# Fewer numerators among gate/up chunks, and a first down pair that projects last: a gated mix of linear attention and a GEGLU block

## Chip, cores, metric

One core of one Trainium2 chip. The metric is device time in microseconds of one execution. Profile times are microseconds from the start of the profiled span, which is about 1.3 us shorter than the device time. In profile lines PE is TensorE's matmuls, PEld its weight loads, DVE VectorE, ACT ScalarE, SPq SyncE issuing a DMA, and L726 line 726 of the kernel.

## The reference, cut to what matters

```
x: (1, 2048, 640) bf16; 32 heads of 20; F = 1728
g = sigmoid((x * gate_w).sum(-1))
a = o @ wo,  o = num / den,  num = phi_q @ kv          # linear attention, phi = softmaxes of +pq and -pq
b = (gelu(x @ w_gate) * (x @ w_up)) @ w_down           # GEGLU block
out = g * a + (1 - g) * b
```

Of the kernel before, what the change touches and what calls it, by code (L numbers as in the profile page):

```python
# [107 lines left out]
class _Kernel:  # L108
# [6 lines left out]
    NFC = 14  # L115
# [235 lines left out]
    def mm(self, bank, c0, n, lhs, rhs, first, fin, reads):  # L351

        for a, z in ((0, 64), (64, P)) if self.columns else ((0, P),):
            self.sc.op("pe", lambda e: e.matmul(  # L354
                self.ps[a:z, bank * 512 + c0:bank * 512 + c0 + n], lhs[:, a:z], rhs, start=first, stop=fin),
                reads=reads, writes=[("ps", bank)], signal=fin and z == P)
# [345 lines left out]
        sc.dma("sp", lambda e: e.dma_start_transpose(self.goT[:, gs, :, :], self.Og[:, sl, :]),  # L702
               reads=[("Og", sl)], writes=[("goT", gs)], guard=old)

    def down_pair(self, t0, banks, widths):

        sc = self.sc
        ts = (t0, t0 + 1)
        NFC, KD = self.NFC - 1, self.KD
        nw = len(widths)  # L710
        hk = t0 // 4
        last = t0 + 2 == self.NT
        os_ = t0 % 4

        def mm(r, j, h, c, opens, x, n):
            t = ts[j]
            tt, gs, bk, w0, a = t % 4, t % 8, banks[h][j], sum(widths[:h]), 64 * r
            w, end = widths[h], x == n - 1
            if c <= NFC:
                lhs, rhs = self.hT(hk, c)[a:a + 64, tt * P:(tt + 1) * P], self.wd_sb[a:a + 64, c, w0:w0 + w]  # L720
                rd = [("hT", hk, c), "wd"] if c < NFC else [("hT", hk, 13, r), ("wd13", r)]
            else:
                k = c - NFC - 1
                lhs, rhs = self.goT[a:a + 64, gs, k, :], self.wo_sb[a:a + 64, k, w0:w0 + w]
                rd = [("goT", gs), "wo"]
            sc.op("pe", lambda e: e.matmul(self.bank(bk, w), lhs, rhs, start=opens and x == 0, stop=end and not opens,  # L726
                                           skip_group_check=True),
                  reads=rd, writes=[("ps", bk)] + ([("turn", bk)] if end else []), signal=end,
                  after=[("turn", bk)] if x == 0 and not opens else ())

        def evac(h):
            w0, w = sum(widths[:h]), widths[h]
            for j in (0, 1):
                bk, dst, g = banks[h][j], self.outsb[:, os_ + j, w0:w0 + w], self.Gm[:, ts[j]:ts[j] + 1]
                rd, wr = [("ps", bk), "Gm"], [("outsb", os_ + j, h)]
                if last and j == 1:
                    sc.op("dve", lambda e: e.tensor_scalar(dst, self.bank(bk, w), g, None, op0=ALU.mult), reads=rd, writes=wr)
                else:
                    sc.op("act", lambda e: e.activation(dst, self.bank(bk, w), AF.Copy, scale=g), reads=rd, writes=wr)  # L739
            if last:  # L740
                hs, c0, c1 = [h], w0, w0 + w
            elif h == nw - 1:
                hs, c0, c1 = range(nw), 0, self.D
            else:
                return
            if t0 < self.TB:
                rows = self.out[0:self.BT, :].rearrange("(p j) n -> p j n", j=self.TB)[:, t0:t0 + 2, :]
            else:
                rows = self.out[t0 * P:(t0 + 2) * P, :].rearrange("(j p) n -> p j n", p=P)
            sc.dma("sp", lambda e: e.dma_start(rows[:, :, c0:c1], self.outsb[:, os_:os_ + 2, c0:c1]),  # L750
                   reads=[("outsb", os_ + j, k) for j in (0, 1) for k in hs], writes=[("out", t0, h)])

        wos = [NFC + 1 + k for k in range(KD)]
        opening = list(range(NFC + 1)) + wos
        for part in (range(NFC + 1), range(NFC + 1, len(opening))):
            for h in range(nw):
                for x in part:
                    for r in (0, 1):
                        mm(r, r, h, opening[x], True, x, len(opening))
                    yield None  # L760
        closing = list(range(NFC)) + wos
        for h in range(nw):
            for x, c in enumerate(closing):
                for r in (0, 1):
                    mm(r, 1 - r, h, c, False, x, len(closing))
                if c == closing[-1]:
                    evac(h)
                yield None

    NUMB = 2  # L770
    oldk = [("Ek", k, r) for k in range(4) for r in (0, 1)] + [(w, k) for w in ("Dk", "Rk") for k in range(4)] + [
# [3 lines left out]
    def ffn(self):  # L775
        self.gn = 0
        self.pn = 0
        pairs = [(0, 1), (6, 7)]

        def gateups(b, after):  # L780
            for idx, c in enumerate([0, 1, 13] + list(range(2, 13))):
                self.gateup(b, c, pairs[self.pn % 2])
                self.pn += 1
                after(idx)

        def downs(b, side):
            p = [pairs[(self.pn + k) % 2] for k in (0, 1)]
            n = 0
            for t in (4 * b, 4 * b + 2):
                final = t + 2 == self.NT  # L790
                for _ in self.down_pair(t, p + [(2, 3)] if final else p, (256, 256, 128) if final else (320, 320)):
                    n += 1
                    if n in side:
                        self.num(side[n])

        def state(idx):
            if idx < 3:
                self.gram(13 + idx)
            if idx == 2:
                self.columns = False  # L800
                self.kv_evac()
                self.gates()
                self.kv_ones()
            if 6 <= idx < 11:
                self.kv_mask(idx - 6)

        def first_nums(idx):
            if idx in (4, 8):
                self.num(idx // 4 - 1)

        def none(idx):
            pass
        at = (1, 31, 61, 91)
        gateups(0, state)
        gateups(1, first_nums)
        gateups(2, none)
        gateups(3, none)
        for b in range(self.NB):
            downs(b, {at[k]: 4 * b + 2 + k for k in range(4 if b < 3 else 2)})


def bass_gated_mix__linear_kernel_hedgehog__geglu_ffn__prompt_kernel(
# [41 lines left out]
```

## The kernel before, where the change touches it

After the attention state is built, the kernel runs four blocks of gate/up (512 tokens each, matmuls over all 128 rows), then four down phases of four 128-token tiles. A *numerator* is what one tile needs of `phi_q @ kv`: 20 matmuls over 64 rows into PSUM banks 2 to 5, eleven VectorE instructions that end in `Og`, and one DMA transpose of `Og` into `goT`. The output projection of that tile (`wo` steps) reads `goT`.

A down phase has two *tile pairs* of 74 *steps* each. A step is two matmuls of 64 rows and 320 columns, one in each row half of TensorE, working at the same time on two PSUM banks. In the second half of a pair the row halves swap tiles, and so banks. A matmul that enters a swapped bank waits until the other half's last one there is complete (`after=turn`).

```
# numerators: two among gate/up block 1, the others inside down phases
def first_nums(idx):
    if idx in (4, 8):
        self.num(idx // 4 - 1)
at = (1, 31, 61, 91)
for b in range(self.NB):
    downs(b, {at[k]: 4 * b + 2 + k for k in range(4 if b < 3 else 2)})   # step -> tile

# one tile pair (down_pair): steps 0..NFC are down, wos the output projection
opening = list(range(NFC + 1)) + wos
for part in (range(NFC + 1), range(NFC + 1, len(opening))):
    for h in range(nw):                  # h: which bank pair (320 columns each)
        for x in part:
            for r in (0, 1):
                mm(r, r, h, opening[x], True, x, len(opening))
            yield None
closing = list(range(NFC)) + wos
for h in range(nw):
    for x, c in enumerate(closing):
        for r in (0, 1):
            mm(r, 1 - r, h, c, False, x, len(closing))    # row halves swapped
        if c == closing[-1]:
            evac(h)
        yield None
# ... (cut)
```

The softmax here doesn't subtract the row's maximum and nothing guards it: scores larger than these inputs give would overflow.

## Time and profile before

| | |
|---|---|
| time, median of 6 runs | 287.47 us (287.15 to 288.72) |
| profiled span | 286.2 us, clock 1.000 |
| TensorE busy | 281.8 us (98%), 98% of the chain that ended last |
| numerator among gate/up | costs TensorE 0.60 us |
| numerator in a down phase | costs TensorE 0.39 us |
| step in a down phase | 0.136 us |

TensorE bounds the kernel, and it hardly ever waits. So each instruction added to it, and each wait, goes into the time at full size. Another engine or a DMA matters only where TensorE waits for it. The lines behind the table are in the prediction (timelines: start, duration, what). One more line of the before profile also belongs here: VectorE's timeline at tile 3's sum (columns: start, duration, what, idle time before it and its releaser).

```profile
206.96 0.49 DVE L699 TENSOR_TENSOR Og<-O,O 128x640 bf16<-128x640 bf16 x1 [0.44 <-DVE O L697]
```

Other such sums start 0.09 us after the instruction before them; this one pauses 0.44. Before the change nobody waited for it.

### The profile page before, as it was taken

How to read it: one execution, taken by the hardware profiler on the slowest of the kernel's cores; microseconds unless marked ns; L12 is line 12 of the kernel's file. 1: busy time of each engine (PE TensorE's matmuls, PEld its weight loads, DVE VectorE, ACT ScalarE, POOL GpSimd, SP SyncE). 2: the span in 40 equal slices, each digit the busy share in tenths (PEclk: the TensorE clock that was granted, in tenths of full speed). 3: DMA queues.
4: the chain of work that ended last, by engine and by line, in shares of the span. 5: the costliest groups of instructions: out<-in, count | busy, mean ns of one | idle time of the engine just before them, and what ended most of it. 6: DMA issues, size and time to landing. Idle time of an engine off the chain costs nothing.

```text
span 286.2 us, 7006 instructions
## 1 busy us (share of the span) xinstructions
PE 281.8 (98%) x3017; PEld 186.7 (65%) x3032; DVE 174.9 (61%) x353; ACT 104.5 (37%) x199; POOL 5.3 (2%) x36
## 2 busy tenths in 40 slices
PE   8999999999999999999999999999999999999996
PEld 5566789999994444444444444445777777777785
DVE  2349999999976652567242334225883883883801
ACT  3367897678653222222323223221112112112111
POOL 7000000000000000000000000000000000000000
PEclk9999999999999999999999999999999999999999
DMA  8999996000002000011000000000232132222221
GB/s 226 206 176 236 367 366 201 0 2 2 2 0 48 0 0 0 3 24 23 2 0 0 0 2 0 0 0 2 25 84 62 45 48 81 61 49 72 70 72 48
DMA packets 36937, 18.67 MB, mean 65 GB/s; under 512 B 28970, under 2 KB 36394, under 8 KB 36906
## 3 DMA queue, kind: packets, MB, share of 16 engines
q1 hardware_dynamic: 36240, 18.19, 25.6%
q8 instruction: 24, 0.39, 0.6%
q10 hardware_dynamic: 666, 0.03, 0.2%
q14 instruction: 7, 0.06, 0.1%
HBM read 9.04 MB, written 2.62 MB: 41 GB/s over the span
## 4 chain that ended last, share of the span: by engine, by line
PE 98%; issue 0%; ACT 0%
PE ps L354 61%; PE ps L726 28%; PE ps L670 2%; PE ps L366 2%; PE ps L461 2%; PE ps L334 1%; PE ps L550 1%; PE ps L293 1%; ACT outsb L739 0%; PE ps L316 0%
## 5 line engine op out<-in xcount | busy, mean ns | idle before, releaser
L354 PE MATMUL ps<-xT,wg_sb 128*128 128x512 bf16 (+1 forms) x265 | 63.8, 379 | 0.4 <-issue 0.2
L354 PE MATMUL ps<-xT,wu_sb 128*128 128x512 bf16 (+1 forms) x263 | 63.3, 379 | 0.5 <-DVE hT L644 0.2
L642 ACT ACTIVATE gl<-ps 128x512 bf16<-128x512 f32 x52 | 30.9, 596 | 73.1 <-PE ps L354 68.7
L644 DVE TENSOR_TENSOR hT<-ps,gl 128x512 bf16<-128x512 f32 x39 | 26.7, 690 | 38.6 <-PE ps L354 38.5
L726 PE MATMUL ps<-wd_sb,hT 64*128 64x320 bf16 x648 | 48.5, 296 | 0.0
L354 PEld LDWEIGHTS ps<-xT,wu_sb 128*128 128x128 bf16 (+1 forms) x270 | 26.5, 99 | 29.8 <-DVE hT L644 0.5
L354 PEld LDWEIGHTS ps<-xT,wg_sb 128*128 128x128 bf16 (+1 forms) x270 | 26.2, 99 | 29.0 <-ACT gl L642 0.2
L354 PE MATMUL ps<-w,xT 128*64 128x512 bf16 (+6 forms) x398 | 41.5, 325 | 0.1
L739 ACT ACTIVATE outsb<-ps,Gm 128x320 bf16<-128x320 f32 (+2 forms) x31 | 14.5, 515 | 72.4 <-PE ps L726 72.4
L726 PEld LDWEIGHTS ps<-wd_sb,hT 64*128 64x128 bf16 x648 | 31.1, 94 | 12.2 <-issue 0.4
L354 PEld LDWEIGHTS ps<-w,xT 128*64 128x64 bf16 (+1 forms) x400 | 35.9, 107 | 4.5
L726 PE MATMUL ps<-wo_sb,goT 64*128 64x320 bf16 (+2 forms) x340 | 26.5, 288 | 0.0
L354 PE MATMUL ps<-xT,wq 128*64 128x512 bf16 (+1 forms) x184 | 26.0, 380 | 0.1
L431 DVE TENSOR_REDUCE Dk<-Ek 128x64 f32<-128x1280 bf16 x16 | 23.7, 1479 | 3.6 <-ACT gcol L419 3.6
L445 DVE TENSOR_TENSOR Ek<-Ek,Dk 128x640 bf16<-128x640 bf16 x32 | 25.0, 821 | 0.6
L697 DVE TENSOR_TENSOR O<-ps,RH 128x640 bf16<-128x640 f32 x32 | 24.8, 816 | 0.0
L416 ACT ACTIVATE Ek<-ps 128x640 bf16<-128x640 f32 x32 | 20.7, 703 | 4.2 <-PE ps L354 4.2
L530 ACT ACTIVATE Eq<-ps 128x512 bf16<-128x512 f32 x40 | 21.6, 607 | 0.6 <-PE ps L354 0.4
L644 DVE TENSOR_TENSOR xT<-ps,gl 128x512 bf16<-128x512 f32 x13 | 9.0, 691 | 18.2 <-PE ps L354 18.2
L726 PEld LDWEIGHTS ps<-wo_sb,goT 64*128 64x128 bf16 x340 | 16.0, 94 | 5.3
L354 PEld LDWEIGHTS ps<-xT,wq 128*64 128x64 bf16 (+1 forms) x185 | 15.4, 108 | 2.9
L726 PE MATMUL ps<-wd_sb,xT 64*128 64x320 bf16 (+2 forms) x270 | 16.0, 269 | 0.0
(69 smaller groups left out, 174.8 us busy)
## 6 DMA issues: line engine op xcount, KB each, us to landing
out_dram<-outsb SPq DMA_DIRECT2D x7, 320.0 KB, 2.3
wd_sb<-in_B_w_down_dram SPq DMA_DIRECT2D x1, 2080.0 KB, 13.9
wg_sb<-in_B_w_gate_dram SPq DMA_DIRECT2D x1, 1120.0 KB, 6.2
wu_sb<-in_B_w_up_dram SPq DMA_DIRECT2D x1, 1120.0 KB, 9.8
wg_sb<-in_B_w_gate_dram SPq DMA_DIRECT2D x1, 960.0 KB, 9.8
wu_sb<-in_B_w_up_dram SPq DMA_DIRECT2D x1, 960.0 KB, 10.2
w<-in_A_wqkv_dram SPq DMA_DIRECT2D x5, 160.0 KB, 4.0
wo_sb<-in_A_wo_dram SPq DMA_DIRECT2D x1, 800.0 KB, 9.2
```

What stands on the lines that cost most here:

```text
L354: self.sc.op("pe", lambda e: e.matmul(self.ps[a:z, bank * 512 + c0:bank * 512 + c0 + n], lhs[:, a:z], rhs, start=first, stop=fin), reads=r ...
L366: sc.op("pe", lambda e, c0=c0, n=n, bk=bk, col=col: e.matmul(self.bank(bk)[:, col:col + n], self.xT[:, kt, t * P:(t + 1) * P], self.w3[:, ...
L416: self.sc.op("act", lambda e, s=s, scale=scale: e.activation(self.Ek[:, se, s, :], self.ps[:, o:o + self.D], AF.Exp, scale=scale), reads=[ ...
L431: sc.op("dve", lambda e: e.tensor_reduce(self.Dk[:, se, 0, :].rearrange("p (s h) -> p s h", h=H), self.Ek[:, se, :, :].rearrange("p s (h d ...
L445: sc.op("dve", lambda e, v=v, r=r: e.tensor_tensor(v, v, r, ALU.mult), reads=[("Rk", se)], writes=[("Ek", se, s)])
L461: sc.op("pe", lambda e: e.matmul(self.ps[a:a + 64, b * 512 + c:b * 512 + c + 2 * nf], va[:, lo:lo + 64], self.Ek[:, se, :, f0:f0 + nf], st ...
L530: sc.op("act", lambda e, s=s, scale=scale: e.activation(self.Eq[:, s, i, b * self.BT:(b + 1) * self.BT], self.bank(bank), AF.Exp, scale=sc ...
L642: sc.op("act", lambda e: e.activation(self.gl[:, slot, :], self.bank(banks[0]), AF.Gelu_apprx_tanh), reads=[("ps", banks[0])], writes=[("g ...
L644: sc.op("dve", lambda e: e.tensor_tensor(hT, self.bank(banks[1]), self.gl[:, slot, :], ALU.mult), reads=[("ps", banks[1]), ("gl", slot)], ...
L697: dve(lambda e, o=o, f=f, s=s: e.tensor_tensor(o, V[s][:, :, :, 0:DH], f, ALU.mult), rb + [key(6 + s)], [("O", s, sl)], guard=old)
L726: sc.op("pe", lambda e: e.matmul(self.bank(bk, w), lhs, rhs, start=opens and x == 0, stop=end and not opens, skip_group_check=True), reads ...
L739: sc.op("act", lambda e: e.activation(dst, self.bank(bk, w), AF.Copy, scale=g), reads=rd, writes=wr)
```

## The change

Intent: only one numerator stays among gate/up, where it costs two changes of TensorE's tiling mode. The first down phase takes five numerators. So that tile 1 is in time there, the first tile pair takes all its down steps first and its output projection last ("late").

```
+        down = (list(range(NFC + 1)), list(range(NFC)))
+        def leg(h, half, cs, first, fin, enter, leave):
+            for x, c in enumerate(cs):
+                for r in (0, 1):
+                    mm(r, (r, 1 - r)[half], h, c, first and x == 0, fin and x == len(cs) - 1,
+                       enter and x == 0, leave and x == len(cs) - 1)
+                if fin and x == len(cs) - 1:
+                    evac(h)
+                yield None
+        if late:
+            for half in (0, 1):
+                for h in range(nw):
+                    yield from leg(h, half, down[half], half == 0, False, half == 1, True)
+            for h in range(nw):
+                yield from leg(h, 0, wos, False, False, True, True)
+                yield from leg(h, 1, wos, False, True, True, True)
+        else:
+            ... (the old order, in legs; cut)
...
-                for _ in self.down_pair(t, ..., (256, 256, 128) if final else (320, 320)):
+                for _ in self.down_pair(t, ..., (256, 256, 128) if final else (320, 320), t == 0):
...
-            if idx in (4, 8):
-                self.num(idx // 4 - 1)
+            if idx == 4:
+                self.num(0)
...
-        at = (1, 31, 61, 91)
+        at = (1, 31, 61, 91, 121)
+        nums = ((1, 2, 3, 4, 5), (6, 7, 8, 9), (10, 11, 12, 13), (14, 15))
-            downs(b, {at[k]: 4 * b + 2 + k for k in range(4 if b < 3 else 2)})
+            downs(b, dict(zip(at, nums[b])))
```

More of the change, by code (lines that the diff above doesn't have):

```diff
@@ L703, in num, with down_pair @@
                reads=[("Og", sl)], writes=[("goT", gs)], guard=old)
-    def down_pair(self, t0, banks, widths):
+    def down_pair(self, t0, banks, widths, late):
         sc = self.sc
@@ L713, in down_pair, with mm @@
         os_ = t0 % 4
-        def mm(r, j, h, c, opens, x, n):
+        def mm(r, j, h, c, start, stop, enter, leave):
             t = ts[j]
             tt, gs, bk, w0, a = t % 4, t % 8, banks[h][j], sum(widths[:h]), 64 * r
-            w, end = widths[h], x == n - 1
+            w = widths[h]
             if c <= NFC:
@@ L725, in mm @@
                 rd = [("goT", gs), "wo"]
-            sc.op("pe", lambda e: e.matmul(self.bank(bk, w), lhs, rhs, start=opens and x == 0, stop=end and not opens,
+            sc.op("pe", lambda e: e.matmul(self.bank(bk, w), lhs, rhs, start=start, stop=stop,
                                            skip_group_check=True),
-                  reads=rd, writes=[("ps", bk)] + ([("turn", bk)] if end else []), signal=end,
-                  after=[("turn", bk)] if x == 0 and not opens else ())
+                  reads=rd, writes=[("ps", bk)] + ([("turn", bk)] if leave else []), signal=leave,
+                  after=[("turn", bk)] if enter else ())
         def evac(h):
@@ L753, in down_pair @@
         wos = [NFC + 1 + k for k in range(KD)]
-        opening = list(range(NFC + 1)) + wos
-        for part in (range(NFC + 1), range(NFC + 1, len(opening))):
-            for h in range(nw):
-                for x in part:
-                    for r in (0, 1):
-                        mm(r, r, h, opening[x], True, x, len(opening))
-                    yield None
-        closing = list(range(NFC)) + wos
-        for h in range(nw):
-            for x, c in enumerate(closing):
+        down = (list(range(NFC + 1)), list(range(NFC)))
+        def leg(h, half, cs, first, fin, enter, leave):
+            for x, c in enumerate(cs):
                 for r in (0, 1):
-                    mm(r, 1 - r, h, c, False, x, len(closing))
-                if c == closing[-1]:
+                    mm(r, (r, 1 - r)[half], h, c, first and x == 0, fin and x == len(cs) - 1, enter and x == 0,
+                       leave and x == len(cs) - 1)
+                if fin and x == len(cs) - 1:
                     evac(h)
                 yield None
+        if late:
[6 more added lines that the diff above has]
+        else:
+            for h in range(nw):
+                yield from leg(h, 0, down[0], True, False, False, False)
+            for h in range(nw):
+                yield from leg(h, 0, wos, False, False, False, True)
+            for h in range(nw):
+                yield from leg(h, 1, down[1] + wos, False, True, True, True)
     NUMB = 2
@@ L790, in downs @@
                 final = t + 2 == self.NT
-                for _ in self.down_pair(t, p + [(2, 3)] if final else p, (256, 256, 128) if final else (320, 320)):
+                for _ in self.down_pair(t, p + [(2, 3)] if final else p, (256, 256, 128) if final else (320, 320),
+                                        t == 0):
                     n += 1
```

## The prediction

> **What bounds the kernel now**
>
> I read the page first (busy shares, then the chain that ended last), then the PE timeline around one numerator among gate/up and around those in the first down phase, then the VectorE and SyncE timelines for what a numerator's result goes through.
>
> Page, busy time by engine, and the chain:
>
> ```profile
> PE 281.8 (98%) x3017; PEld 186.7 (65%) x3032; DVE 174.9 (61%) x353; ACT 104.5 (37%) x199; POOL 5.3 (2%) x36
> ...
> PE 98%; issue 0%; ACT 0%
> ```
>
> TensorE is busy 98% of 286.2 us and carries 98% of the chain. The clock row is 9 throughout. So only three things count: TensorE cycles added or removed, and waits of TensorE. There is hardly a wait to win back, so a large gain is excluded from the start: 2% would be 5.75 us.
>
> PE timeline around the numerator that the change takes out of gate/up (the second one there):
>
> ```profile
> 126.91 1.03 PE L354 MATMUL ps<-xT,wu_sb 128*128 128x512 bf16 x4
> 127.87 0.56 PE L670 MATMUL ps<-KV,Eq 64*128 64x88 bf16 x20
> 128.37 0.82 PE L354 MATMUL ps<-xT,wg_sb 128*128 128x512 bf16 x3
> ```
>
> Gate/up matmuls start every 0.216 us (five take 1.24 us, the last of them 0.379). The last one before the numerator starts at 127.56, so without it the next would start at 127.78; it starts at 128.37, and its successor 0.226 instead of 0.216 later. The numerator costs 0.60 us here.
>
> Chain in order of time, first down phase:
>
> ```profile
> 197.61 0.24 PE ps L726 x2
> 197.85 0.39 PE ps L670 x20
> 198.24 4.08 PE ps L726 x60
> 202.32 0.39 PE ps L670 x20
> 202.71 4.07 PE ps L726 x60
> 206.78 0.39 PE ps L670 x20
> 207.18 4.08 PE ps L726 x60
> 211.25 0.39 PE ps L670 x20
> 211.64 7.88 PE ps L726 x116
> ```
>
> There it costs 0.39 us. A "step" (two concurrent 64-row matmuls) takes 4.08 / 30 = 0.136 us. No gap: TensorE waits for nothing, and one numerator to the next is 4.46 us.
>
> What becomes of a numerator (numbers of the one at step 61 of this phase, which is tile 4 before): PE, VectorE, SyncE timelines.
>
> ```profile
> 206.62 0.56 PE L670 MATMUL ps<-KV,Eq 64*128 64x88 bf16 x20
> 207.37 0.36 DVE L686 RECIPROCAL RH<-ps 128x32 f32<-128x32 f32 x1
> 209.44 1.55 DVE L697 TENSOR_TENSOR O<-ps,RH 128x640 bf16<-128x640 f32 x2
> 211.08 0.49 DVE L699 TENSOR_TENSOR Og<-O,O 128x640 bf16<-128x640 bf16 x1
> 211.64 1.20 SPq L702 DMA_TRANSPOSE goT<-Og  x1
> 212.97 0.71 PE L726 MATMUL ps<-wo_sb,goT 64*128 64x320 bf16 x8
> ```
>
> Its four banks are free after 209.44 + 1.55 = 210.99, 4.37 us after its start; its transpose is issued 5.02 us after its start. The sixteen transposes land 2.6 us after issue at the least and in the median, 4.2 at most (those of the first down phase: 3.6, 2.6, 2.6, 2.6). So a tile is ready for the output projection no sooner than 5.02 + 2.57 = 7.59 us after its numerator started. The last line is where the second tile pair of the phase (tiles 2 and 3) begins its output projection.
>
> **What the Trainium skill says**
>
> "TensorEngine Tiling (Array Packing)", Key Properties: a change of tiling mode drains TensorE. Gate/up is 128 rows, numerators and down steps 64, so a numerator among gate/up pays two switches; the trace agrees: 0.60 against 0.39 us. The same page, Gotcha 1, says that row tiles must not access one PSUM bank at the same time and that software must see to it: this is what the wait on "turn" is for, when the two row halves swap banks. "TensorE: Matmul & The Clock Gate", Single matmul latency, gives (398 + N) / 2.4 ns warm, 299 ns for N = 320; the trace's row has 296. "DMA: Bandwidth & Descriptors", the anatomy of one DMA, puts about 2 us of fixed cost on each DMA, mostly the write receipt; the transposes' 2.6 us agree, and say that the landing cannot be hurried.
>
> **The change part by part**
>
> No arithmetic is added or removed: the same sixteen numerators, the same matmuls. ACT's order stays; TensorE, VectorE and SyncE get a new order.
>
> 1. One numerator (tile 1) goes from gate/up into the first down phase: 0.60 - 0.39 = **-0.21 us**. The numerator that stays in gate/up is the one that also makes TensorE wait for VectorE (0.17 us, at 124.5), so that small wait is not won back.
>
> 2. The first tile pair now takes its down steps for both halves, then per bank pair the projection of half 0 directly followed by that of half 1. Half 1 swaps the banks between the row tiles, so its first weight load waits for the last matmul of half 0, just issued. Before, there were always at least five steps (0.68 us) between such a pair, over twice the latency. Estimate: 0.296 (matmul) + 0.054 (semaphore to weight load, as VectorE's end at 124.47 to the load at 124.52) + 0.01 for the unprefetched load, less the 0.136 that would pass anyway: 0.22 to 0.24 each, at steps 60 and 70. Two: **+0.47 us**.
>
> 3. All numerators slip by one place: tile 1 at step 1, 2 at 31, 3 at 61, 4 at 91, 5 at 121. The pair of tiles 2 and 3 still projects from step 103. Before, tile 3 was at 31, 72 steps ahead; now it is at 61. Between lie 41 steps (5.56), the numerator itself and that at step 91 (0.78): 6.34 us, plus the second turn wait 0.24 = 6.58 us. Needed: 7.59 + 0.05 = 7.64. TensorE waits 1.06 us. The same read off the lines above: the transpose of step 61 is issued at 211.64 and lands at 214.21, the projection starts at 212.97 + 0.24. **+1.06 us**.
>
> 4. Five numerators make the distance between the one at step 121 and the first of the next phase 28 steps (27 left of 148, and one): 28 x 0.136 + 0.39 = 4.19 us. The next needs the banks: 4.37 + 0.05 = 4.42 plus a short reload. Every other distance is 30 steps (4.46) or more, which just suffices. **+0.24 us**.
>
> 5. Tile 1 itself: needed from step 55, in the before timeline at 205.67 (its "late" form is there to buy this time); transposed from 202.66, landed at 205.23 if it takes 2.57: slack 0.4. With the 3.6 us that the transpose at that very place took before, TensorE would wait 0.6. In the DMA packets of the trace that transpose overlaps a 16 KB instruction fetch of TensorE (203.4 to 204.7); the slow ones of later phases do so too. One numerator less ahead of the phase puts that fetch 40 instructions later, ten steps (1.36 us), just behind the transpose's packets. I allow a quarter of 0.6: **+0.15 us**.
>
> Tile 5, 55 steps ahead of its use, has 8.5 us: no wait. Evacuation of the first pair's bank pair 0 now ends 10 steps (1.4 us and more) before those banks open again, ACT needs 1.0: no wait.
>
> Sum: -0.21 + 0.47 + 1.06 + 0.24 + 0.15 = +1.71. 287.44 + 1.7 = **289.1 us**, slower by 0.6%.
>
> **The rivals**
>
> A: the order was chosen well and only part 1 and the pairs' waits count, i.e. tile 3 is in time. For it: the "late" form shows that the author minded readiness. Against: it is applied to the first pair alone, and 6.6 us are less than the shortest chain of 7.64 that the trace has. It would give 287.44 - 0.2 + 0.5 + 0.2 = 287.9.
>
> B: transposes run into instruction fetches. 4.2 us in place of 2.57 for tile 3 and 3.6 for tile 1 would add 1.6 and 0.6: 290.6 to 291.2. For it: four of sixteen transposes took 3.9 us or more and three others 3.2 to 3.6. Against: the fetch near step 91 should come after that numerator, about 211.9 to 213.1 with the turn waits, mostly ahead of tile 3's packets (213.1 to 214.0).
>
> C: the mode switch costs more than the gap shows, or the remaining numerator's VectorE wait goes too: at most 0.4 more gained, 288.7.
>
> D: the turn waits are cheaper, because the modelled ends of matmuls overstate the latency. Half of 0.47 goes, but part 3 then waits 0.1 longer: 288.9.
>
> **Range and chances**
>
> Parts 1, 2 and 4 are uncertain by some 0.3 us together, part 3 by -0.3 and +1 (fetch), and runs of the same kernel on another chip by about 0.3. So 288.1 to 290.3 at 8 in 10, with more room above than below. To be 2% faster 5.75 us would have to go, of which TensorE has nothing to give; 2% slower takes three waits as large as part 3. Faster 0.005, within 2% 0.98, slower 0.015.
>
> **What would show it right or wrong**
>
> The PE chain of the changed kernel should have: one numerator in gate/up at the same 0.6 us, and 0.6 us less in gate/up; two gaps of 0.1 us or less in busy time, seen as 0.37 instead of 0.14 between starts, inside the first pair's projection; a wait of about 1 us of the projection of tiles 2 and 3 for the transpose (busy time shows some 0.2 less of it, as ends are modelled); about 0.2 us before the first numerator of the second down phase, released by VectorE's line 697 (or its new number). Second to fourth phases keep 21.7 us each. If no wait stands before tiles 2 and 3's projection, part 3 is wrong and rival A holds; if it is 2 us or more, rival B does; if the span falls, my account of what TensorE waits for is wrong altogether.

## The result, and the profile after

290.93 us in the median of 6 runs (290.58 to 292.26), against 287.47 of before: slower, clear of noise, though by less than 2%; ratio 1.0115 (95% interval 1.0087 to 1.0143). The direction was right; the size was not: +3.5 us instead of +1.7, and above the range's upper end of 290.3.

The TensorE timeline of the changed kernel in the first down phase (columns as before; lines left out):

```profile
196.78 0.56 PE L670 MATMUL ps<-KV,Eq 64*128 64x88 bf16 x20
...
204.76 0.30 PE L726 MATMUL ps<-wo_sb,goT 64*128 64x320 bf16 x1
206.02 1.35 PE L726 MATMUL ps<-wo_sb,goT 64*128 64x320 bf16 x13 [0.96 <-DMA goT<-Og]
207.21 0.56 PE L670 MATMUL ps<-KV,Eq 64*128 64x88 bf16 x20
...
213.83 0.30 PE L726 MATMUL ps<-wo_sb,goT 64*128 64x320 bf16 x1
215.48 1.53 PE L726 MATMUL ps<-wo_sb,goT 64*128 64x320 bf16 x19 [1.36 <-DMA goT<-Og]
```

Two waits for transposes stand here. At 204.76 the first row half, which needs tile 0, starts its projection alone; the second, which needs tile 1, starts at 206.02. Normally the two start 0.003 us apart, so TensorE lost 1.25 us. At 213.83 the same happens with tiles 2 and 3: 1.65 us. (The brackets say less, because a matmul counts as busy until its modelled end.)

The waits of TensorE in the changed kernel that the list of before did not have (waiter <- released by: us in all, times, longest; other lines left out):

```profile
PEld ps L726 <- DMA goT<-Og: 3.0, 2, 1.7
PE ps L726 <- DMA goT<-Og: 2.3, 2, 1.4
PEld ps L726 <- PE ps L726: 0.8, 2, 0.4
PEld ps L670 <- DVE O L697: 0.4, 1, 0.4
```

The third line is the two bank-swap waits. In the starts of the matmuls they are gaps of 0.356 and 0.387 us where 0.133 to 0.136 is usual: 0.22 and 0.25 lost. The fourth is the numerator after the one at step 121, whose banks VectorE had not yet emptied: 0.333 instead of 0.136, 0.20 lost.

VectorE at tile 3's sum, and the chain that ended last from there, in order of time (start, us, what):

```profile
212.01 0.49 DVE L699 TENSOR_TENSOR Og<-O,O 128x640 bf16<-128x640 bf16 x1 [0.44 <-DVE O L697]
```

```profile
211.58 0.43 issue
212.01 0.51 DVE Og L699
...
212.58 2.86 DMA goT<-Og
215.44 0.04 issue
215.48 2.66 PE ps L726 x37
```

The chain now runs through the pause of 0.43 us, the sum and the transpose, before it reaches TensorE. It is the same pause, at the same tile, as before; now somebody waits for it.

The query for the transpose of tile 1 alone answers with its time from issue to landing, first in the changed kernel:

```profile
L702 SPq DMA_TRANSPOSE goT<-Og x1: 1202/1202/1202, 201.8 to 201.8; - x1
...
  PEld ps L726: 1.3, 1
  PE ps L726: 1.0, 1
...
DMA to landing us min/median/max: 4.2/4.2/4.2
```

It was issued at 201.82 and landed at 205.97. This is what the DMA queues started between 203.95 and 204.95: one 16 KB packet of instructions, and three small packets.

```profile
## 3 DMA queue, kind: packets, MB, share of 16 engines
q8 instruction: 1, 0.02, 5.8%
q1 hardware_dynamic: 3, 0.00, 0.6%
```

The profile does not name the engine that the 16 KB packets are for. They are taken for TensorE's, because one comes for every 255 of its instructions in the mean. In the trace's packets this fetch starts 2.14 us after the transpose's issue and takes 0.94. Each transpose has 672 small packets of its own. Undisturbed they run from 1.17 to 2.12 us after issue, and the transpose lands 0.43 to 0.51 us after the last. Here 669 of them had started by 2.13; the last three are those in the view, and they started 3.06 to 3.10 us after issue, as the fetch ended. The transpose landed 1.03 us after the last of them. So 1.0 of its 1.6 us of delay is packets that came only behind the fetch; why the landing then took another 0.5 longer, the trace does not show.

The account of the two profiled runs, in us: numerator out of gate/up -0.60; the same numerator in the down phase +0.39; tile 1's wait +1.25; bank swaps +0.47; tile 3's wait +1.65; numerator at the phase's end +0.20. That is +3.36. In this run the changed kernel reached its first numerator 0.30 sooner and its last output store was 0.14 shorter, which change from run to run. Total +2.9; the spans (289.2 and 286.2) differ by 3.0.

### The profile page after: what moved, and what is told of

It is laid out like the page before. It is cut to its first block, busy times and chain, and to the rows that moved or that the text cites. A ratio compares the mean times of both kernels' runs of the same rounds, so it can differ in the third digit from the quotient of the medians. Undisturbed runs are those within 1.5% of the kernel's fastest.

```text
span 289.2 us, 7022 instructions
## 1 busy us (share of the span) xinstructions
PE 283.3 (98%) x3032; PEld 186.3 (64%) x3032; DVE 175.1 (61%) x353; ACT 104.6 (36%) x199; POOL 5.3 (2%) x36
## 3 DMA queue, kind: packets, MB, share of 16 engines
HBM read 9.04 MB, written 2.62 MB: 40 GB/s over the span
## 5 line engine op out<-in xcount | busy, mean ns | idle before, releaser
L354 PE MATMUL ps<-xT,wg_sb 128*128 128x512 bf16 (+1 forms) x270 | 64.9, 379 | 0.0
L354 PE MATMUL ps<-xT,wu_sb 128*128 128x512 bf16 (+1 forms) x270 | 64.8, 379 | 0.0
L726 PE MATMUL ps<-wd_sb,hT 64*128 64x320 bf16 x648 | 48.8, 296 | 0.0
L726 PEld LDWEIGHTS ps<-wd_sb,hT 64*128 64x128 bf16 x648 | 31.4, 94 | 12.1 <-issue 0.4
L726 PE MATMUL ps<-wo_sb,goT 64*128 64x320 bf16 (+2 forms) x340 | 27.4, 288 | 2.5 <-DMA goT<-Og 2.3
L726 PEld LDWEIGHTS ps<-wo_sb,goT 64*128 64x128 bf16 x340 | 16.0, 94 | 8.9 <-DMA goT<-Og 3.0
L726 PE MATMUL ps<-wd_sb,xT 64*128 64x320 bf16 (+2 forms) x270 | 16.0, 269 | 0.0
```

The lines of the kernel that those rows point to most:

```text
L354: self.sc.op("pe", lambda e: e.matmul(self.ps[a:z, bank * 512 + c0:bank * 512 + c0 + n], lhs[:, a:z], rhs, start=first, stop=fin), reads=r ...
L726: sc.op("pe", lambda e: e.matmul(self.bank(bk, w), lhs, rhs, start=start, stop=stop, skip_group_check=True), reads=rd, writes=[("ps", bk)] ...
```

## The experiments

Two theories of tile 1's 4.2 us were set against each other. F: a fetch of TensorE's instructions that falls into a transpose delays its landing. P: the first transpose of a down phase is slow at that place, whatever fetches do. Instructions added to TensorE's warm-up at the very start shift all later fetches without changing any work that counts: in the warm-up the engine only runs while the first loads arrive. "Tile 1's wait" and "tile 3's wait" below are excess gaps between the starts of TensorE's matmuls in the profiled run.

### Fetches shifted

```
-for n in (512, 512, 512, 512, 512, 512, 128):      # warm-up matmuls, columns each
+for n in (64,) * 50:                               # shift86: 86 instructions more
+for n in (128,) * 25:                              # shift36: 36 more
+for n in (32,) * 100:                              # shift186: 186 more
+for n in (512, 512):                               # warm2: 10 fewer
```

Control, the kernel before with 86 more:

> The kernel before with TensorE's warm-up in 50 matmuls of 64 columns instead of 7 of up to 512: 86 instructions more ahead of everything, no other work. A control. Theory F (a 16 KB instruction fetch of TensorE that falls between about 0.4 and 2.2 us after a transpose's issue delays its landing) and theory P (the first transpose of a down phase is slow at that place whatever the fetch does) both expect the time of before, 287.4 within 0.4 us, as nothing waits there. F: the first transpose of the first down phase (tile 2) lands 2.6 us after issue instead of 3.6. P: 3.6 again.

287.44 us, ratio 1.0003 (0.9981 to 1.0026): the edit costs nothing. The transpose of tile 2, first in its down phase, landed after 2.60 us; in the unedited kernel before it took 3.57, with a fetch 0.78 us after its issue. Now the fetch came 1.4 us ahead of the issue. Same place, other landing: P falls.

> The changed kernel with the same 86 instructions. The fetch that fell 2.1 us after the issue of tile 1's transpose should come 21 steps (2.9 us) sooner, 0.8 us ahead of it. F: tile 1 lands after 2.6 us instead of 4.15, no wait before the first projection (was 1.25 us); tile 3 lands after 2.6 instead of 2.86, wait 1.35 instead of 1.65; time 289.4 instead of 290.9. P: tile 1 again 4.1 us, time 290.9.

289.77 us, ratio 1.0079 (1.0053 to 1.0104). The fetch came sooner, but by 1.3 us and not 2.9: it now started 0.86 us after the issue. Tile 1 landed after 3.39 us, its wait fell from 1.25 to 0.50, tile 3's to 1.38. F's direction holds; my assumption that a fetch is tied to a fixed instruction does not.

> The changed kernel with the warm-up in 25 matmuls of 128: 36 instructions more. The fetch comes 9 steps (1.2 us) sooner: 0.9 us after the issue of tile 1's transpose, before its first packets and overlapping them. F: tile 1 lands after 3.6 to 4.2 us, wait 0.7 to 1.25; tile 3 after 2.6, wait 1.35; time 290.1 to 290.6. P: 290.9 with both landings as in the changed kernel.

289.54 us, ratio 1.0077 (1.0055 to 1.0099). Fetch 0.60 us after the issue, taking 1.45; landing 3.67, tile 1's wait 0.78, tile 3's 1.46. As F has it, though the time fell a little more than expected (its down phases started 0.6 us sooner than those of the run above, as that run reached its first numerator sooner).

> The changed kernel with the warm-up in 100 matmuls of 32 columns: 186 TensorE instructions more, nearly one whole fetch (256), so the next fetch should fall near 70 instructions (2.4 us) later than in the changed kernel: 4.5 us after the issue of tile 1's transpose. F: tile 1 lands after 2.6, no wait; tile 3 after 2.6, wait 1.35; time 289.4, provided that the short warm-up matmuls do not delay the start. P: 4.15 and 1.25 again, 290.9.

289.13 us, ratio 1.0059 (1.0032 to 1.0085). No fetch from 3.6 us before to 4.8 us after the issue of tile 1's transpose, which landed after 2.62. Its query (same view as above):

```profile
L702 SPq DMA_TRANSPOSE goT<-Og x1: 1202/1202/1202, 202.5 to 202.5; - x1
...
DMA to landing us min/median/max: 2.6/2.6/2.6
```

Tile 1's wait is gone, and the waits list has one for a transpose where the changed kernel had two:

```profile
PEld ps L726 <- DMA goT<-Og: 1.4, 1, 1.4
PE ps L726 <- DMA goT<-Og: 1.1, 1, 1.1
```

This run settles the largest error of the prediction. The work, its order and the step at which tile 1 is used are those of the changed kernel; only the warm-up and with it the fetch are elsewhere, and 1.25 us are back. (That such a warm-up costs nothing by itself was tested with 86 instructions, not with 186.)

> The changed kernel with 2 warm-up matmuls instead of 7: 10 instructions fewer ahead, so the fetch comes 0.3 us later, 2.4 to 2.5 us after the issue of tile 1's transpose. In all runs so far fetches up to 2.31 us after an issue made the landing 4.0 to 4.4 us and those from 2.32 on left it at 2.6. F with that edge: tile 1 lands after 2.6, no wait there (1.25 us gone), though the fetch overlaps more of the landing than before. A softer F (any overlap before landing delays): still 3.5 or more. P: 4.15. The time may lose up to 0.5 us at the start for the shorter warm-up: 289.4 to 290.2.

291.97 us, ratio 1.0152 (1.0115 to 1.0189). Inconclusive for what it was made for: the fetch did not move past 2.3 us but came 2.12 us after the issue, and tile 1 landed after 4.27 (wait 1.38). At tile 3 another fetch came 1.16 us after its issue, beside an output store: landing 3.65, wait 2.45. So the time rose where a fall was expected. Between the profiled runs (292.53 and 290.58) half of the rise is in the two waits, for a reason that F covers; the other half is that this one reached its first numerator 0.9 us later.

The 14 profiled kernels, those below included, hold 224 of these transposes. Sorted by where the first 16 KB fetch starts, from 1.5 us before to 4.3 us after a transpose's issue:

| fetch starts, us after issue | transposes | landing min / median / max, us |
|---|---|---|
| before the issue | 18 | 2.55 / 2.58 / 3.58 |
| 0 to 0.3 | 4 | 2.64 / 2.71 / 2.81 |
| 0.3 to 0.7 | 33 | 2.86 / 3.18 / 4.37 |
| 0.7 to 1.06 | 10 | 3.27 / 3.59 / 4.27 |
| 1.06 to 2.31 | 41 | 2.58 / 4.17 / 5.08 |
| 2.32 to 4.3 | 44 | 2.54 / 2.58 / 4.55 |
| none near | 74 | 2.55 / 2.60 / 3.59 |

A fetch that starts while the packets run, or up to 0.2 us after the time when undisturbed ones have ended (2.12), costs most: 1.6 us. The long ones among "before the issue" and "none near" (11 of 3.2 us, 4 of 3.6) had an 8 KB fetch of another queue at about 2.0 us. The edge in time is not sharp: one fetch at 2.29 did nothing, one at 2.50 came with 4.55.

The packets separate the cases better than the clock does. In 38 of the 41 cases of the fifth row no other DMA's small packets mix in. In 37 of these at least two packets of the transpose ran only as the fetch ended; the other one is that of 2.29, which had none left. Of the 44 cases of the sixth row, one alone had packets left, two of them: that of 2.50. And in all 117 cases, of whatever row, in which every packet had run by 2.14 us after issue, the landing came after 2.54 to 2.63. This was found in the traces afterwards; no run was made to test it.

### VectorE's instructions shifted

```
+for _ in range(12):
+    sc.op("dve", lambda e: e.memset(self.gtmp[:, 1:2], 0.0), writes=["gpad"])   # at the very start
```

> As the changed kernel with 86 TensorE instructions, and 12 tiny memsets of VectorE at its start. VectorE pauses 0.44 us before tile 3's sum, in before and after alike. If that pause is its own instruction buffer being refilled at a fixed instruction, it moves 12 instructions up, into tile 2's numerator, where there is slack: tile 3's wait falls from 1.35 to 0.9 and the time is 289.0. If it belongs to tile 3's place (another wait), the pause stays and the time is 289.4.

288.93 us, ratio 1.0048 (1.002 to 1.0077). Tile 3's sum in this run's VectorE timeline has no pause any more (the experiments with memsets have two lines more, so L699 is L701 there):

```profile
211.44 0.49 DVE L701 TENSOR_TENSOR Og<-O,O 128x640 bf16<-128x640 bf16 x1
```

Tile 3's wait fell from 1.38 to 1.02 us, while tile 1's rose from 0.50 to 0.61 with its fetch, so the traces explain 0.25 us of the 0.8 by which the median fell. In all eleven profiled kernels without the memsets the pause stands before the same instruction of VectorE, this sum; in the three with them it does not. So it belongs to a place in VectorE's instruction stream, not to a wait of tile 3. Where it went is not shown: it can hide in VectorE's next wait for TensorE. That it is a refill of its instructions is argued from this and from an 8 KB instruction packet near it, not shown.

### Parts of the change alone

```
late_only:  after.py with   if idx in (4, 8): self.num(idx // 4 - 1)   and   nums = ((2, 3, 4, 5), ...)
nums_only:  -  ..., t == 0):      +  ..., False):
late2:      -  ..., t == 0):      +  ..., t < 4):
legs:       -  for h in range(nw):
            -      yield from leg(h, 0, wos, False, False, True, True)
            -      yield from leg(h, 1, wos, False, True, True, True)
            +  for half in (0, 1):
            +      for h in range(nw):
            +          yield from leg(h, half, wos, False, half == 1, True, True)
```

> The kernel before with the new order of steps in the first tile pair and nothing else: tiles 0 and 1 stay among gate/up, four numerators in the first down phase at their old places. Account of the waits (A): only the two bank-swap waits come, 0.22 and 0.25 us, no wait for a transpose: time of before + 0.5 = 287.9, ratio 1.0016. Rival (R): the order itself costs more, for instance an evacuation late for the next pair: 1 us or more.

287.90 us, ratio 1.0004 (0.9984 to 1.0024). The trace shows the two bank-swap gaps, 0.387 us each (0.25 lost), and no wait for a transpose. By the clock 0.5 us is within this interval; the gaps carry the verdict.

> The changed kernel without the new order of steps: tile 1's numerator at step 1, its projection at step 29. A: 4.2 us of work lie between, 7.6 (no fetch in the way) to 9.2 are needed: a wait of 3.4 to 5.0 us there, tile 3 waits 1.0 to 1.7 more, no bank-swap wait; time 292.0 to 294.0, slower than the changed kernel. R (the order is what costs the time): about 289.

294.40 us, ratio 1.0214 (1.018 to 1.0249; whether it is over 2% is unclear). The waits are as A has them, but the time is 0.4 above its range, for a reason that A had not foreseen (below). Tile 1's wait was 3.64 us even with a clean landing of 2.62: no fetch came near, which fits that TensorE uses up no instructions while it stands. After so long a wait TensorE ran at half its clock for a while. The stretches of this run (from:to, length, busy time of each engine, granted clock, DMA):

```profile
201.50:205.00 3.50, 0.26 (x3) 0.00 (x0) 0.76 (x2) 0.00 (x0) 0.00 (x0) 0.96 0.24 47
205.00:208.00 3.00, 2.89 (x38) 2.11 (x40) 0.93 (x4) 0.00 (x0) 0.00 (x0) 0.50 0.00 0
```

Steps took 0.26 us instead of 0.136 there, about ten of them. Three of the four runs have a mean clock of 0.994 and took 294.3 to 294.5; the fourth, at 1.000, took 292.62, within A's range. So the late order was needed: without it the numerators' move costs some 3.5 us more, or 1.7 where the clock holds (one run).

> The changed kernel with the new order of steps in both tile pairs of the first phase, so that tile 3 is needed at step 129 instead of 103. A: tile 3's wait (1.65 us) goes, two bank-swap waits more (0.47), which also give the numerator at the phase's end its banks in time (0.2 gained); tile 1's wait of 1.25 stays, as the fetch falls at the same instruction: 290.9 - 1.65 + 0.47 - 0.2 = 289.5. R: 291.4, if the waits for tile 3 only move to the later step.

289.94 us, ratio 1.0071 (1.005 to 1.0092). Tile 3's wait is gone although its transpose took 3.27 us this time; four bank-swap waits of 0.22 to 0.25; no wait at the phase's end; tile 1's wait is there as before (fetch 2.19 us after issue, landing 4.18, wait 1.28). Each term is as expected; the time is 0.4 above A's sum, and far from R's. The profiled run reached its first numerator 0.7 us later than that of before.

> The changed kernel with the four projection legs of the first pair reordered: half 0 on both bank pairs, then half 1 on both, so that five steps lie between two uses of a bank by swapped row halves. A: no bank-swap wait (0.47 gained); the first bank pair is evacuated five steps (0.68 us) before it opens again, ACT needs 1.0: a new wait of 0.3 to 0.4; tile 1's wait stays, tile 3's about the same: 290.7 to 290.9. R: if the swap waits cost nothing, 291.2.

291.23 us, ratio 1.0128 (1.0102 to 1.0154). The bank-swap waits are gone and 0.38 us of waiting for ScalarE's evacuation came in their place. It is in the waits list:

```profile
PEld ps L726 <- ACT outsb L739: 0.6, 2, 0.3
```

Tile 1's transpose again met a fetch (2.31 us after issue, landing 4.37, wait 1.47), tile 3's wait was 1.57. The time alone is the one that R names; the trace decides against R, as the two gaps of the swaps are gone and others of 0.38 us stand for them. Swap waits are real, and the obvious way around them costs nearly the same.

### Versions that might beat both

> All waits for transposes taken away from the changed kernel at once: the new order of steps in both tile pairs of the first phase, 186 TensorE instructions more ahead (as in the run that cleared tile 1), and 12 VectorE memsets. A: no wait for a transpose, none of the numerator at the phase's end, none in gate/up; four bank-swap waits of 0.25 remain: 287.5 - 0.21 - 0.17 + 1.0 = 288.1, still not below the kernel before. If the numerator moved out of gate/up were worth more than 0.2 us (rival): 287.5 or less.

287.83 us in 6 runs, ratio 1.0018 (0.9999 to 1.0038). The only new wait left in its list is that of the bank swaps:

```profile
PEld ps L728 <- PE ps L728: 1.7, 4, 0.4
```

Tile 3's transpose took 4.44 us here, and nobody waited. With all waits for DMA gone, the change is level with the kernel before or a little behind it: what it saves, 0.21 us, is less than the swaps cost. By the clock this is within noise; in the profiled runs first numerator to last matmul took 165.76 us here and 165.03 before.

> The kernel before with 12 tiny memsets of VectorE at its start, the one cheap gain that the runs point to: VectorE's pause in the numerator among gate/up moves away, and TensorE's 0.17 us wait at 124.5 should go: 287.3 against 287.45, ratio 0.9994, within noise by the clock but visible as a gap in the trace. Rival: the pause stays at that place, gap and time as before.

287.20 us in 6 runs, ratio 0.9993 (0.9974 to 1.0013). TensorE's wait of 0.17 us in gate/up is gone from the trace (weight load and matmul there start on time), and the median is 0.4 lower than that of the same rounds. By the interval it is the same time. It is the fastest version tried, but not shown to be faster.

## Why the prediction was right or wrong

| step of the prediction | predicted | measured in the changed kernel | |
|---|---|---|---|
| 1, numerator out of gate/up | -0.21 | -0.60 + 0.39 = -0.21 | right |
| 2, bank-swap waits | +0.47 | +0.22 + 0.25 | right; alone 0.25 each |
| 3, tile 3 waits | +1.06 | +1.65 | right place, too small |
| 4, numerator at the phase's end | +0.24 | +0.20 | right |
| 5, tile 1 | +0.15 | +1.25 | wrong |
| sum | +1.71 | +3.36 | |

Step 5 failed, in its cost. The prediction had seen that an instruction fetch lies over the slow transpose of the kernel before, and that one numerator less would bring the fetch 1.36 us later, "just behind the transpose's packets". The fetch did come 1.37 us later, at 2.14 us after issue, when the packets of an undisturbed transpose have just ended. But the prediction took that place for nearly out of the way and allowed a quarter of 0.6 us. In fact three packets were not through and ran only as the fetch ended, so the transpose landed after 4.15 us and TensorE waited 1.25 instead of 0.15. That is worse than the overlap of before (3.57). The profile of before held the warning: its first transpose of the third down phase has a fetch 2.12 us after its issue, five packets that came behind it, and landed after 4.18.

Step 3 was right in mechanism and 0.6 too small, by two terms. One is VectorE's pause, which belongs to tile 3. The prediction took its chain, 5.02 us from numerator to issue, from the numerator at the same step in the kernel before. That was tile 4, which starts where the pause has passed; tile 3's chain took 5.37. The other is a fetch 0.35 us after tile 3's issue, which made its landing 2.86 instead of 2.57. 0.35 and 0.29 make the 1.65 within 0.05. Shifted fetches (1.39) and the moved pause (1.02) take them away again.

Of the rivals, B (fetches) had the right cause and expected 290.6 to 291.2, but I gave it too little weight. That the time lies in its range is partly luck: B put the landing of 4.2 us at tile 3 and 3.6 at tile 1, while tile 1 took 4.15 and tile 3 2.86, and the pause, which B did not have, made up part of the difference. Its sign, a wait of 2 us or more before tiles 2 and 3 project, did not come (1.65). A (only swaps) is refuted by the waits; C (a dearer mode switch) by the 0.60 saved in gate/up, where VectorE's wait stayed; D (cheaper swaps) by the gaps. The 0.296 us of a matmul in step 2 is line L726's mean in the page of before, from modelled ends; the gaps of 0.356 and 0.387 bear out the estimate made from it (0.36).

What stays open: what makes a fetch start when it does. Between two fetches of the kernel before, 185 to 337 instructions of TensorE start (weight loads, matmuls and waits; mean about 255), and 86 more at the start moved the fetch at tile 1 of the changed kernel by 41 and that at tile 2 of the kernel before by 92. Open too is why a landing after held packets comes later after the last packet (1.03 against 0.43 to 0.51 us). I could not place a fetch to 0.3 us, so the edge at 2.3 us was seen but not tested on purpose. Packets were recorded in profiled runs only. That the same fetch met tile 1 in the other five runs is inferred from their times.

## What to carry to other kernels

When an order is tightened so that a DMA's landing sets a wait, budget the landing with what else the DMA engines may carry, the engines' own instruction fetches among them, and not with the median of a kernel in which nobody waited. The chain to take from the old profile is that of the same tile, not of the same place, because pauses can belong to a position in an engine's instruction stream. And a saving of two tiling switches (0.2 us) does not pay for one wait on a bank that the other row half has just left (0.25 us), nor for one transpose that is needed less than 7.6 us after its numerator starts (5.0 us chain and 2.6 us transpose), or 9.2 us where a fetch costs it the usual 1.6.

## What the Trainium skill lacked or had wrong

- "Runtime: NRT & Kernel Launch", Instruction fetch mechanics, has the sequencer fetch blocks of 16 KiB (256 instructions) over a DMA queue of its own, with a cost that is "mostly hidden". The 16 KB packets and their mean spacing of 255 instructions agree. Neither it nor "DMA: Bandwidth & Descriptors", which tells under Queues, rings and completion order that each DMA engine takes its queues in turn, packet by packet, says what such a fetch costs a data DMA in flight: a transpose of 2.6 us landed after 4.2 us in the median when a fetch started 1.06 to 2.31 us after its issue (41 cases), which cost this kernel 1.25 us.
- "DMA: Bandwidth & Descriptors", Anatomy of one DMA, has its breakdown for DMAs issued from GpSimd alone. For the transposes here, issued from SyncE, the trace has the first packet 1.17 us after issue, the last one's end at 2.12 and the landing 0.43 to 0.51 later when undisturbed; with all disturbances they landed after 2.54 to 5.08 us, and most of the spread goes with instruction fetches.
- No page read for this has the pause of 0.44 us that VectorE showed at one place of its instruction stream, and that was gone from there with 12 added instructions.
- "TensorEngine Tiling (Array Packing)", Key Properties, has the drain at a mode switch but no size. Two switches cost 0.21 us here (0.60 against 0.39 for the same numerator). Gotcha 1 there leaves the wait between row tiles on one bank to software; that wait measured 0.22 to 0.25 us for 320 columns.
